# Attention steps two at a time beside an MLP: a changed instruction order on TensorE

## The chip, the cores and the metric

The kernel runs on one core of a Trainium2 chip. The metric is the time of one execution on the device in microseconds; the median of several runs counts. The core has five engines with an instruction queue each: TensorE (PE, matrix products into the eight banks of PSUM), VectorE (DVE), ScalarE (ACT), GpSimd (POOL) and SyncE (SP, which issues most DMAs). Each engine takes its instructions in their order; semaphores let it wait for the others.

## The reference

A linear attention with positive random features, and a gated MLP on what it gives. Cut to what matters (8 batches, 8 heads, 576 rows, head size 64, 128 features; 4608 rows of 512 into the MLP, which has 1536 inner columns):

```python
def phi(x):                       # x is q or k, scaled by 1/64**0.25
    proj = einsum('bhsd,md->bhsm', x, omega)
    h = proj - sum(x * x, -1, keepdims=True) / 2
    return exp(h - max(h, -1, keepdims=True)) / sqrt(m)
q_p, k_p = phi(q_s), phi(k_s)
kv = einsum('bhsm,bhsd->bhmd', k_p, v)
z = sum(k_p, axis=2)
x = einsum('bhsm,bhmd->bhsd', q_p, kv) / (einsum('bhsm,bhm->bhs', q_p, z)[..., None] + 1e-6)
x = x.transpose(0, 2, 1, 3).reshape(4608, 512)
g, val = x @ w_gate, x @ w_val
out = (g * sigmoid(g) * val) @ w_out
```

## The kernel before

**Attention.** q and k are cut into groups of 256 rows of a pair of heads (a batch has 8 such groups, and a ninth for the rows that are left over). A *step* takes two groups, mostly one of q and one of k; there are 72 steps. A step n goes through these functions, some of them one to three steps later:

- `st_transpose` turns the two groups on TensorE (tile `pt`, four transposes, in the bank of `ps_tr`); ACT copies the result to `x`, POOL squares the rows (`sq`).
- `st_project` multiplies by omega: eight matmuls into the two banks `pp0` and `pp1`, a bank for each head of the pair (L464). All float32 matmuls that are no transposes leave two records in the trace, so `pp` shows 16 records for a step.
- `st_max` takes sums and maxima on DVE (`st`), `st_exp` the exponentials on ACT (`ph`, eight instructions, which read `pp0` and `pp1`).
- `k_accumulate` adds the k group of two steps before to `kvacc` (one bank); when a half batch is complete, `kv_finalize` copies it to `kvr`. For batches from 4 on it also turns the sums z (`zp`, in the bank of `ps_att`), which go to DRAM and come back spread over the partitions (`load_z`).
- q of batches 0 to 3: `q_transpose` (`ptq`, copied to `qt`), `q_mult` (`po` = features times kv; DVE divides into `xn`), `q_out` (`xt`, two transposes of `xn`).
- q of batches 4 to 7: `q_den` (POOL and DVE: the denominators), `q_norm` (POOL: features divided), `q_transpose`, `q_out` (`xt`, matrix products of kv and `qt`, no transpose of `xn`).
- `q_out` ends with copies of `xt`: into the MLP's input tiles, or for later row tiles to DRAM (`xo`, then `xs`).

**MLP.** `stream` yields it in groups of matmuls on float32r numbers, each 128x512, split into high and low parts: 12 for a `g` or `v` bank, 9 for an `o` bank. They use three banks (`ps_moe`). Behind the attention a second stage follows (`pair_rounds`, seven products for eight) with other PSUM pools. All other time of the weights' conversion (`convert_all`, "ticks") lies on ACT, DVE, POOL and SP.

**PSUM.** Of eight banks the MLP has three, `ps_proj` two, `ps_att`, `ps_tr` and `kvacc` one each.

**Order.** The code is written as a loop over steps; a scheduler then puts the instructions of each engine in an order of its own by priority (the place in the program) and by when it takes operands and buffers to be ready, so the order on an engine isn't that of the code. For the first 25 steps (`EARLY`) the list `CLOSE` gives the order of the functions; there is no MLP work yet. From step 25 on it is the list `GROUPED`: attention functions, with `SHARE` at six places, where a share of the MLP groups that are due in this step is given out. `course` says how much MLP is due at which step.

Of the kernel before, what the change touches and what calls it, by code (L numbers as in the profile page):

```python
# [11 lines left out]
F32 = mybir.dt.float32  # L12
# [12 lines left out]
def kernel(  # L25
# [404 lines left out]
    def st_transpose(n):  # L430
# [12 lines left out]

        st = att.tile([P, 4, 2, CH, 2], F32, name=f"st_{n}", tag="st", bufs=6)
        sq = att.tile([P, 2, CH, 2, D], F32, name=f"sq_{n}", tag="sq")
# [12 lines left out]
    def st_project(n):  # L458
        if n >= NS:
            return  # L460
        x, st, sq = sts[n]

        new = ps_moe if n < EARLY and n % 2 else ps_proj
        pp = [new(f"pp{hh}_{n}", [P, 2, CH, M]) for hh in range(2)]  # L464
        for i in range(2):
            for c in range(CH):
                for hh in range(2):
                    r = slice(hh * D, (hh + 1) * D)
                    matmul(
                        pp[hh][:, i, c, :], x[r, i, c * P : (c + 1) * P], omT[r], start=True, stop=True  # L470
                    )
        sts[n] = st, sq, pp
        return True
# [44 lines left out]
    def kv_finalize(b, a2):  # L518
        acc = kvacc.pop((b, a2))
        raw = att.tile([P, 4, VW], F32, name=f"kvr{b}_{a2}", tag="kvr", bufs=4)  # L520
        nc.scalar.copy(raw, acc)  # L521
        for j in range(2):
            kvst[b, 2 * a2 + j] = raw[:, 2 * j : 2 * j + 2, :]
        if b >= BPOOL:

            zp = ps_att(f"zp{b}_{a2}", [4, P])
            transpose(zp, raw[:, :, D], ident)
            zs = att.tile([4, P], F32, name=f"zs{b}_{a2}", tag="zs")
# [5 lines left out]
    zds = {}  # L534
    zbc = {}
# [14 lines left out]
    def q_den(n):  # L550

        n -= JLAG
        for _, b, g, gr in slots(n, "q"):
# [10 lines left out]
            else:  # L564
# [4 lines left out]
                )  # L569
            dn = att.tile([P, 3, CH, 2], F32, name=f"dj{b}_{g}", tag="dj", bufs=6)  # L570
            nc.vector.tensor_reduce(dn[:, 0], jk, axis=AX.X, op=ALU.add)  # L571
# [63 lines left out]
    def q_mult(n):  # L635

        n -= MLAG
        for _, b, g, gr in slots(n, "q"):
# [17 lines left out]
            nc.vector.reciprocal(dn[:, 1], dn[:, 0])  # L656
            xn = att.tile([P, CH, 2, D], F32, name=f"xn{b}_{g}", tag="jx")
            nc.vector.tensor_tensor(
# [14 lines left out]
    def q_out(n):  # L673
        n -= OLAG
        for i, b, g, gr in slots(n, "q"):
            po = (ps_att if n + OLAG < EARLY or i else ps_tr)(f"xt{b}_{g}", [P, G])
            first = column(b, gr)
# [4 lines left out]
            else:  # L682
# [3 lines left out]
                for pr, o, w in segs:  # L686
                    for hh in range(2):
                        matmul(
                            po[hh * D : (hh + 1) * D, o : o + w], kvst[b, pr][:, hh, 0:D], qt[:, hh, o : o + w],
                            start=True, stop=True, skip_group_check=True,  # L690
                        )
            j, o = tile_of(first)
            if gr is None:
# [17 lines left out]
            if gr is None or gr[0] == NPAIR - 1:  # L711
                cols_done[0] = first + (RES if gr is None else G)
        return bool(slots(n, "q"))

# [405 lines left out]
    def turn_next(n):  # L1120
# [48 lines left out]
    ends = []  # L1169
    for n in range(NN):  # L1170
        if loaded <= n + LA:
# [6 lines left out]
        if n == FIRST_RAW:  # L1178
            load_raw(0)
        want = OPS * np.interp(clock[n + 1], [clock[m] for m, _ in marks], [x for _, x in marks])  # L1180
        order = CLOSE if n < EARLY else GROUPED
        left = len(order) if n < EARLY else order.count(SHARE)
        for what in order:
            with ExitStack() as es:
                if n < EARLY:
                    for ins in ends if what is st_project else ends[:1]:
                        es.enter_context(tc.issue_after(ins.ins))
                if what is not SHARE:
                    what(n)
            if n < EARLY:  # L1190
                if what is st_project:
                    ends.clear()
                ends.append(newest_pe[0])
            if what is turn_next and n < 2:
                warm(2, turned_in[0])
            if n < EARLY or what is SHARE:
                due = course[n + 1] - given[0] - debt[0]
                if due > 0:
                    give(due / left)
                for _ in range(int(np.ceil((want - ticks[0]) / left))):  # L1200
                    tick()
                left -= 1
        load_z(n)
    late.close()
    for name, pool in (
# [39 lines left out]
```

## Time and profile before

| | |
|---|---|
| runs (3) | 1166.57 to 1167.58 us, median 1166.86 us |
| profiled execution | 1166.82 us, span from first to last instruction 1165.0 us |
| mean granted TensorE clock | 0.997 of full |
| instructions in the trace | 18915 |
| DMA | 114.30 MB, mean 98 GB/s |

The profile page gives the busy time of each engine, the groups of instructions and the chain of work that ended last. The timeline lists instructions in order of time: start in microseconds from the span's start, duration, engine, line, operation, output and inputs, count, and in brackets how long the engine was idle before it and what ended that. TensorE's durations overlap with the next instruction's, so a piece of work there is measured from its start to the start of the next.

### The profile page before, as it was taken

Reading aid. Unit: us, or ns where it says so; the run is one execution under the profiler, and the core shown is the slowest. Engines: PE = TensorE matmul, PEld = TensorE weight load, DVE = VectorE, ACT = ScalarE, POOL = GpSimd, SP = SyncE. Lnnn points to the kernel's source line nnn. Section 1 sums busy time; section 2 is a strip of 40 time slices with the busy share of each in tenths; the row PEclk is TensorE's granted clock in tenths of the full one; section 3 lists DMA queues with packets and bytes.
Section 4 is the critical chain, followed back from the end, with each engine's and each line's share of the span. In section 5 each row is a group of like instructions: output and inputs, shape, how many; then the busy total and the mean of one; then the engine's idle time right before and its main releaser. Section 6 shows DMA issues by size and latency. Waiting matters only on the chain.

```text
span 1165.0 us, 18915 instructions
## 1 busy us (share of the span) xinstructions
PE 1137.2 (98%) x6645; PEld 939.5 (81%) x6646; DVE 707.4 (61%) x1289; ACT 678.3 (58%) x1539; POOL 615.5 (53%) x559
## 2 busy tenths in 40 slices
PE   8999999999999999989999999999999999999998
PEld 6888888888878778867788778888878888888886
DVE  5787667455656656565474566665566666456654
ACT  5887886876776866757434544454544445444441
POOL 5664433344556675587245555544455543455551
PEclk9999999999999999999999999999999999999999
DMA  6764445655445642322544111124211111211103
GB/s 137 179 160 114 128 142 161 178 135 143 122 126 137 168 132 78 114 68 65 154 118 126 46 55 55 55 74 122 59 55 55 54 37 46 81 55 55 46 19 72
DMA packets 173966, 114.30 MB, mean 98 GB/s; under 512 B 125840, under 2 KB 144304, under 8 KB 173872
## 3 DMA queue, kind: packets, MB, share of 16 engines
q1 hardware_dynamic: 172528, 112.78, 35.5%
q8 instruction: 52, 0.85, 0.3%
q10 hardware_dynamic: 1344, 0.33, 0.1%
q14 instruction: 42, 0.34, 0.1%
HBM read 87.88 MB, written 25.18 MB: 97 GB/s over the span
## 4 chain that ended last, share of the span: by engine, by line
PE 74%; DVE 10%; ACT 6%; POOL 4%; DMA 3%; issue 2%; SPq 1%; ACTq 0%; POOLq 0%; DVEq 0%
PE o L103 22%; PE a L103 16%; PE c L103 8%; PE g L103 6%; PE pp L103 4%; PE v L103 4%; PE d L103 4%; PE kvacc L103 3%; ACT ph L505 3%; PE ptq L107 2%; PE po L103 2%; PE pt L107 2%; PE xt L103 1%; DVE st L490 1%; POOL wlo L264 1%
## 5 line engine op out<-in xcount | busy, mean ns | idle before, releaser
L505 ACT ACTIVATE ph<-pp,st 128x128 f32<-128x128 f32 x576 | 157.8, 386 | 26.5 <-DVE st L493 26.0
L763 DVE TENSOR_TENSOR acc<-o,acc 128x512 f32<-128x512 f32 x156 | 105.8, 684 | 94.6 <-PE o L103 94.3
L446 POOL TENSOR_TENSOR sq<-nat 128x512 f32<-128x512 f32 x72 | 78.2, 1086 | 130.5 <-DVE st L483 89.1
L950 POOL TENSOR_TENSOR wlo<-wspare,whi 128x512 fp32r<-128x512 f32 (+1 forms) x60 | 61.0, 1037 | 117.4 <-ACT whi L949 111.0
L490 DVE TENSOR_REDUCE st<-pp 128x4 f32<-128x512 f32 x144 | 92.5, 683 | 39.0 <-PE pp L103 38.7
L264 POOL TENSOR_TENSOR wlo<-wraw,whi 128x512 fp32r<-128x512 f32 x59 | 82.7, 1406 | 26.7 <-ACT whi L263 22.8
L103 PE MATMUL pp<-omT,x 64*128 64x128 f32 x1152 | 87.3, 285 | 3.2 <-ACT x L454 2.2
L103 PEld LDWEIGHTS pp<-omT,x 64*128 64x128 f32 x1152 | 72.6, 187 | 20.2 <-issue 11.2
L950 POOL TENSOR_TENSOR wlo<-s,whi 128x512 fp32r<-128x512 f32 x64 | 82.6, 1311 | 3.8 <-ACT whi L949 3.8
L1059 ACT COPY late<-a 128x512 f32<-128x512 f32 x72 | 42.2, 586 | 59.7 <-PE a L103 58.5
L103 PE MATMUL o<-whi,late 128*128 128x512 f32 x192 | 74.5, 389 | 0.0
L571 DVE TENSOR_REDUCE dj<-jk 128x4 f32<-128x512 f32 x36 | 24.6, 684 | 73.5 <-POOL jk L567 60.6
L103 PE MATMUL kvacc<-v,ph 128*128 128x65 f32 x512 | 65.9, 268 | 0.5 <-ACT kvr L521 0.5
L824 POOL TENSOR_TENSOR hl<-sl,hh 128x512 fp32r<-128x512 f32 x36 | 47.0, 1308 | 34.8 <-ACT hh L823 34.7
L103 PEld LDWEIGHTS kvacc<-v,ph 128*128 128x128 f32 x512 | 63.1, 192 | 0.8 <-ACT kvr L521 0.6
L1063 DVE TENSOR_TENSOR late<-c,late 128x512 f32<-128x512 f32 x25 | 17.3, 692 | 69.7 <-PE c L103 60.6
L103 PE MATMUL g<-xh,whi 128*128 128x512 f32 x144 | 59.4, 412 | 0.0
L103 PE MATMUL o<-whi,hh 128*128 128x512 f32 x144 | 58.5, 406 | 0.1
L303 POOL TENSOR_TENSOR wc<-st 128x512 int32<-128x512 int32 x36 | 37.5, 1042 | 39.6 <-DVE st L298 17.2
L103 PE MATMUL v<-xh,whi 128*128 128x512 f32 x144 | 57.9, 402 | 0.0
L103 PE MATMUL g<-xh,wlo 128*128 128x512 f32 x144 | 57.7, 401 | 0.0
L103 PE MATMUL g<-xl,whi 128*128 128x512 f32 x144 | 57.2, 397 | 0.0
(261 smaller groups left out, 3369.4 us busy)
## 6 DMA issues: line engine op xcount, KB each, us to landing
wraw<-wscr SPq DMA_DIRECT2D x63, 256.0 KB, 2.7
wspare<-wscr SPq DMA_DIRECT2D x60, 256.0 KB, 2.8
wscr<-wc SPq DMA_DIRECT2D x36, 256.0 KB, 2.2
out_dram<-acc SPq DMA_DIRECT2D x72, 128.0 KB, 2.4
nat<-in_k_dram SPq DMA_DIRECT2D x64, 128.0 KB, 3.0
nat<-in_q_dram SPq DMA_DIRECT2D x64, 128.0 KB, 3.1
v<-in_v_dram SPq DMA_DIRECT2D x62, 128.0 KB, 3.5
st<-in_moe_w_gate_dram SPq DMA_DIRECT2D x12, 512.0 KB, 4.1
```

Source lines behind the costliest of these rows:

```text
L103: newest_pe[:] = [nc.tensor.matmul(*args, **kw)]
L107: newest_pe[:] = [nc.tensor.transpose(*args, **kw)]
L264: nc.gpsimd.tensor_tensor(lo, raw, hi.bitcast(F32), op=ALU.subtract)
L303: nc.gpsimd.tensor_tensor(ui, ri, low, op=ALU.add)
L446: nc.gpsimd.tensor_tensor(sq, nat, nat, op=ALU.mult)
L490: nc.vector.tensor_reduce(st[:, 1, :, :, hh], pp[hh], axis=AX.X, op=ALU.max, negate=True)
L505: step_end["s"] = nc.scalar.activation(ph[:, c, hh * M : (hh + 1) * M], pp[hh][:, i, c, :], AF.Exp, bias=st[:, 3, i, c, hh : hh + 1], scal ...
L571: nc.vector.tensor_reduce(dn[:, 0], jk, axis=AX.X, op=ALU.add)
L763: nc.vector.tensor_tensor(a_, po, a_, op=ALU.add)
L824: nc.gpsimd.tensor_tensor(hl, h, hh.bitcast(F32), op=ALU.subtract)
L950: nc.gpsimd.tensor_tensor(lo, src_, hi.bitcast(F32), op=ALU.subtract)
L1059: newest["s"] = nc.scalar.copy(keep[name], ps)
```

## The change

From step 25 on the loop goes over two steps at a time with one list, `DOUBLE`, whose entries are a function and which of the two steps it is called for. Its head puts together: `q_out` of both steps (`q_out_both`, two groups in one bank of `ps_moe`), `st_project` of both steps, `k_accumulate` of both. Behind it come the other functions, with `SHARE` at ten places: the transposes (`q_transpose`, `st_transpose`) now stand between MLP groups. The projections of the first step go to the banks of `ps_att` and `ps_tr`, those of the second to `ps_proj`, so that four banks hold them. `zp` gets a function of its own (`z_rows`), called behind two shares. Buffers: `st` and `dj` 4 for 6, `zs` 1 for 2, `xn` gets a tag of its own. In `CLOSE` the extra `q_out` of step 24 goes, and the transposes of step 26 are called there.

```diff
-        new = ps_moe if n < EARLY and n % 2 else ps_proj
-        pp = [new(f"pp{hh}_{n}", [P, 2, CH, M]) for hh in range(2)]
+        if n < EARLY:
+            new = (ps_moe, ps_moe) if n % 2 else (ps_proj, ps_proj)
+        else:
+            new = (ps_proj, ps_proj) if (n - EARLY) % 2 else (ps_att, ps_tr)
+        pp = [new[hh](f"pp{hh}_{n}", [P, 2, CH, M]) for hh in range(2)]
...
         if b >= BPOOL:
-
+            zraw[b, a2] = raw
+    def z_rows():
+        for (b, a2), raw in zraw.items():
             zp = ps_att(f"zp{b}_{a2}", [4, P])
             transpose(zp, raw[:, :, D], ident)
...
     def q_out(n):
-        n -= OLAG
-        for i, b, g, gr in slots(n, "q"):
-            po = (ps_att if n + OLAG < EARLY or i else ps_tr)(f"xt{b}_{g}", [P, G])
+        place_out([(g_, (ps_att if n < EARLY else ps_tr)(f"xt{g_[1]}_{g_[2]}", [P, G])) for g_ in slots(n - OLAG, "q")])
+    def q_out_both(n):
+        groups = slots(n - 1 - OLAG, "q") + slots(n - OLAG, "q")
+        at = []
+        for k_, g_ in enumerate(groups):
+            if k_ % 2 == 0:
+                two = ps_moe(f"xt{g_[1]}_{g_[2]}", [P, 2, G])
+            at.append((g_, two[:, k_ % 2]))
+        place_out(at)
...
-        lambda n: n == EARLY - 1 and q_out(n),
         lambda n: n == EARLY - 1 and q_mult(n),
+        lambda n: n == EARLY - 1 and st_transpose(n + 2),
...
-    GROUPED = (
-        q_out,
-        st_project,
-        q_transpose,
-        lambda n: k_accumulate(n, 0),
-        lambda n: k_accumulate(n, 1),
-        st_max,
-        st_exp,
-        q_den,
-        lambda n: st_transpose(n + 1),
-        SHARE, SHARE, SHARE,
-        lambda n: q_norm(n + 1),
-        q_mult,
-        SHARE, SHARE, SHARE,
-    )
+    DOUBLE = (
+        (q_out_both, 0),
+        (st_project, 0),
+        (st_project, 1),
+        (lambda n: k_accumulate(n, 0), 0),
+        (lambda n: k_accumulate(n, 1), 0),
+        (lambda n: k_accumulate(n, 0), 1),
+        (lambda n: k_accumulate(n, 1), 1),
+        (st_max, 0), (st_exp, 0), (q_norm, 0),
+        SHARE, SHARE,
+        (lambda n: z_rows(), 0), (load_z, 0), (load_z, 1),
+        (q_transpose, 0),
+        (st_max, 1), (st_exp, 1), (q_den, 0),
+        SHARE, SHARE,
+        (st_transpose, 2), (q_norm, 1), (q_mult, 0),
+        SHARE, SHARE, SHARE,
+        (q_transpose, 1), (st_transpose, 3), (q_den, 1),
+        SHARE, SHARE,
+        (q_mult, 1),
+        SHARE, SHARE, SHARE,
+    )
...
+    for n in range(EARLY, NN, 2):
+        loads(n)
+        loads(n + 1)
+        left = DOUBLE.count(SHARE)
+        last = min(n + 2, NN)
+        for what in DOUBLE:
+            if what is not SHARE:
+                what[0](n + what[1])
+                continue
+            share(course[last] - given[0] - debt[0], wanted(last), left)
+            left -= 1
```

What this makes of the order on TensorE, at three places. First the end of the projections of step 47. In the kernel before (`pp` the projection, `ptq` and `pt` the transposes, `v_4` an MLP group):

```order
L103 MATMUL pp_47_4314<-omT,x_4268 128x128
L103 MATMUL pp_47_4315<-omT,x_4268 128x128
L107 MATMUL ptq_3_4324<-ident,ph_45_4137 128x128 x4
L103 MATMUL kvacc_1_4127<-v_102,ph_45_4142 128x65 x4
L107 MATMUL pt_4356<-ident,nat_4088 128x128 x4
L103 MATMUL v_4_4372<-xh_1327,whi_1_3437 128x512
```

In the changed kernel eight rows of `pp_47` are followed by eight of `pp_48`; the last two of these and what follows:

```order
L103 MATMUL pp_48_4325<-omT,x_4258 128x128
L103 MATMUL pp_48_4326<-omT,x_4258 128x128
L103 MATMUL kvacc_1_4126<-v_102,ph_45_4145 128x65 x4
L103 MATMUL kvacc_1_4126<-v_103,ph_46_4193 128x65 x4
L103 MATMUL v_4_4365<-xh_1327,whi_1_3434 128x512
L103 MATMUL v_4_4365<-xl_1328,whi_1_3434 128x512
```

The transposes have left the stretch, and the accumulation of two steps stands in it. Second, where the transposes of the pair of steps 59 and 60 went, inside the MLP groups `o_2_0` and `o_2_1` (TensorE, changed kernel):

```order
L103 MATMUL o_2_0_5728<-wlo_2_5496,hh_8_5560 128x512
L103 MATMUL o_2_0_5728<-whi_2_5495,hl_8_5561 128x512
L107 MATMUL ptq_7_5741<-ident,ph_58_5453 128x128 x4
L103 MATMUL o_2_1_5771<-whi_2_5487,hh_6_5470 128x512
L103 MATMUL o_2_1_5771<-wlo_2_5488,hh_6_5470 128x512
L107 MATMUL pt_5748<-ident,nat_5577 128x128 x4
L103 MATMUL o_2_1_5771<-whi_2_5487,hl_6_5471 128x512
L103 MATMUL o_2_1_5771<-whi_2_5491,hh_7_5517 128x512
```

The same `ptq_7` and its neighbours before the change, at the end of the stretch of step 60:

```order
L107 MATMUL ptq_7_5712<-ident,ph_58_5543 128x128 x4
L103 MATMUL kvacc_0_5618<-v_98,ph_58_5548 128x65 x4
L107 MATMUL pt_5747<-ident,nat_5496 128x128 x4
L103 MATMUL o_2_0_5763<-whi_2_5460,hh_6_5443 128x512
L103 MATMUL o_2_0_5763<-wlo_2_5461,hh_6_5443 128x512
L103 MATMUL o_2_0_5763<-whi_2_5460,hl_6_5444 128x512
```

`ptq_7` now stands between two MLP groups, and `pt` inside one. Third, the first use of a bank of the first projection behind the stretch of steps 33 and 34 (TensorE, changed kernel; `ptq_8` goes to the bank of `ps_att`, which `pp_33` held):

```order
L103 MATMUL kvacc_0_2584<-v_98,ph_31_2599 128x65 x4
L103 MATMUL kvacc_0_2584<-v_99,ph_32_2637 128x65 x4
L103 MATMUL o_0_0_2859<-whi_2_2010,hh_0_2701 128x512
L103 MATMUL o_0_0_2859<-wlo_2_2011,hh_0_2701 128x512
L103 MATMUL o_0_0_2859<-whi_2_2010,hl_0_2702 128x512
L107 MATMUL ptq_8_2832<-ident,ph_32_2632 128x128 x4
L103 MATMUL o_0_0_2859<-whi_2_2064,hh_1_2736 128x512
```

Before, the same transposes followed the projection of step 33 at once, into a bank that no projection uses:

```order
L103 MATMUL pp_33_2773<-omT,x_2696 128x128
L107 MATMUL ptq_8_2782<-ident,ph_32_2681 128x128 x4
L103 MATMUL kvacc_0_2671<-v_98,ph_31_2581 128x65 x4
L107 MATMUL pt_2808<-ident,nat_2533 128x128 x4
L103 MATMUL o_0_0_2830<-whi_2_2036,hh_0_2703 128x512
```

Three MLP matmuls and the accumulation of two steps are now what stands between the projections and the next user of the bank.

More of the change, by code (lines that the diff above doesn't have):

```diff
@@ L524, in kv_finalize @@
         if b >= BPOOL:
+            zraw[b, a2] = raw
+    zraw = {}
+    zds = {}
+    def z_rows():
+        for (b, a2), raw in zraw.items():
             zp = ps_att(f"zp{b}_{a2}", [4, P])
             transpose(zp, raw[:, :, D], ident)
-            zs = att.tile([4, P], F32, name=f"zs{b}_{a2}", tag="zs")
+            zs = att.tile([4, P], F32, name=f"zs{b}_{a2}", tag="zs", bufs=1)
             nc.scalar.copy(zs, zp)
@@ L532, in kv_finalize @@
             zds[b, a2] = zd
-    zds = {}
+        zraw.clear()
     zbc = {}
@@ L569, in q_den @@
                 )
-            dn = att.tile([P, 3, CH, 2], F32, name=f"dj{b}_{g}", tag="dj", bufs=6)
+            dn = att.tile([P, 3, CH, 2], F32, name=f"dj{b}_{g}", tag="dj", bufs=4)
             nc.vector.tensor_reduce(dn[:, 0], jk, axis=AX.X, op=ALU.add)
@@ L656, in q_mult @@
             nc.vector.reciprocal(dn[:, 1], dn[:, 0])
-            xn = att.tile([P, CH, 2, D], F32, name=f"xn{b}_{g}", tag="jx")
+            xn = att.tile([P, CH, 2, D], F32, name=f"xn{b}_{g}", tag="xn")
             nc.vector.tensor_tensor(
@@ L673, in q_out, with place_out @@
     def q_out(n):
-        n -= OLAG
-        for i, b, g, gr in slots(n, "q"):
-            po = (ps_att if n + OLAG < EARLY or i else ps_tr)(f"xt{b}_{g}", [P, G])
+        place_out([(g_, (ps_att if n < EARLY else ps_tr)(f"xt{g_[1]}_{g_[2]}", [P, G])) for g_ in slots(n - OLAG, "q")])
[7 more added lines that the diff above has]
+        place_out(at)
+    def place_out(at):
+        for (i, b, g, gr), po in at:
             first = column(b, gr)
@@ L691, in q_out @@
                         )
+        for (i, b, g, gr), po in at:
+            first = column(b, gr)
             j, o = tile_of(first)
@@ L1134 @@
         q_den,
-        lambda n: n == EARLY - 1 and q_out(n),
         lambda n: n == EARLY - 1 and q_mult(n),
+        lambda n: n == EARLY - 1 and st_transpose(n + 2),
     )
-    GROUPED = (
-        q_out,
-        st_project,
-        q_transpose,
-        lambda n: k_accumulate(n, 0),
-        lambda n: k_accumulate(n, 1),
-        st_max,
-        st_exp,
-        q_den,
-        lambda n: st_transpose(n + 1),
+    DOUBLE = (
[6 more added lines that the diff above has]
+        (lambda n: k_accumulate(n, 1), 1),
+        (st_max, 0),
+        (st_exp, 0),
+        (q_norm, 0),
+        SHARE,
+        SHARE,
+        (lambda n: z_rows(), 0),
+        (load_z, 0),
+        (load_z, 1),
+        (q_transpose, 0),
+        (st_max, 1),
+        (st_exp, 1),
+        (q_den, 0),
+        SHARE,
+        SHARE,
+        (st_transpose, 2),
+        (q_norm, 1),
+        (q_mult, 0),
         SHARE,
@@ L1150 @@
         SHARE,
-        lambda n: q_norm(n + 1),
-        q_mult,
+        (q_transpose, 1),
+        (st_transpose, 3),
+        (q_den, 1),
+        SHARE,
+        SHARE,
+        (q_mult, 1),
         SHARE,
@@ L1169, with loads @@
     ends = []
-    for n in range(NN):
+    def loads(n):
+        nonlocal loaded
         if loaded <= n + LA:
@@ L1179, with share, wanted @@
             load_raw(0)
[L1180 to L1183, printed above, removed]
-            with ExitStack() as es:
[L1185 to L1193, printed above, removed]
+    def share(due, want, left):
+        if due > 0:
+            give(due / left)
+        for _ in range(int(np.ceil((want - ticks[0]) / left))):
+            tick()
+    def wanted(n):
+        return OPS * np.interp(clock[n], [clock[m] for m, _ in marks], [x for _, x in marks])
+    for n in range(EARLY):
+        loads(n)
+        for at, what in enumerate(CLOSE):
+            with ExitStack() as es:
+                for ins in ends if what is st_project else ends[:1]:
+                    es.enter_context(tc.issue_after(ins.ins))
+                what(n)
+            if what is st_project:
+                ends.clear()
+            ends.append(newest_pe[0])
             if what is turn_next and n < 2:
                 warm(2, turned_in[0])
[L1196 to L1202, printed above, removed]
-        load_z(n)
+            share(course[n + 1] - given[0] - debt[0], wanted(n + 1), len(CLOSE) - at)
+        load_z(n)
+    for n in range(EARLY, NN, 2):
+        loads(n)
+        loads(n + 1)
[7 more added lines that the diff above has]
+            left -= 1
     late.close()
```

3 lines of the change are left out of this document (1 added, 2 removed).

## The prediction

> **What bounds the kernel now.** I read the page first, then the stretches of time, then TensorE's waits, then its timeline.
>
> ```profile
> PE 1137.2 (98%) x6645; PEld 939.5 (81%) x6646; DVE 707.4 (61%) x1289; ACT 678.3 (58%) x1539; POOL 615.5 (53%) x559
> PE 74%; DVE 10%; ACT 6%; POOL 4%; DMA 3%; issue 2%; SPq 1%; ACTq 0%; POOLq 0%; DVEq 0%
> ```
>
> TensorE is busy for 98% of the span, and 74% of the chain that ended last lies on it. No other engine is over 61%. So what counts is how many microseconds TensorE's own row of instructions takes, and how long it waits.
>
> ```profile
> 110.00:564.00 454.00, 441.71 (x3030) 359.11 (x3030) 267.69 (x569) 326.00 (x789) 253.43 (x223) 1.00 0.45 125
> ```
>
> This is the stretch from 110 to 564 us (busy time of PE, PEld, DVE, ACT, POOL). By the order of the instructions, TensorE's rows are the same before and after the change up to a place at 110 us and again from 24 MLP matmuls behind 564 us on. So the change is worth what happens in the 454 us between. ACT, the next engine there, is busy for 326 of them (72%): it has room on the mean, not at each moment.
>
> ```profile
> PE ptq L107 <- ACT xo L703: 2.9, 4, 2.1
> PE xt L107 <- DVE xn L658: 2.3, 2, 1.2
> PE zp L107 <- ACT kvr L521: 2.0, 3, 1.1
> PE pt L107 <- ACT qt L633: 1.9, 1, 1.9
> ...
> PE pt L107 <- DVE xl L710: 0.2, 1, 0.2
> ```
>
> TensorE's waits in that stretch are nine groups; these are the four largest (9.1 us) and the last, and all nine come to **12.1 us**. The largest belong to attention steps that wait for a copy out of a PSUM bank.
>
> **What a step costs now.** This is TensorE's timeline around one step whose output is a matrix product (start, duration):
>
> ```profile
> 401.82 0.39 PE L103 MATMUL o<-whi,hl 128*128 128x512 f32 x1
> 402.14 0.65 PE L103 MATMUL xt<-qt,kvr 128*64 128x256 f32 x4
> 402.72 1.16 PE L103 MATMUL pp<-omT,x 64*128 64x128 f32 x16
> 403.82 0.66 PE L107 MATMUL ptq<-ident,ph 128*128 128x128 f32 x4
> 404.31 1.00 PE L103 MATMUL kvacc<-v,ph 128*128 128x65 f32 x8
> 405.15 0.61 PE L107 MATMUL pt<-ident,nat 128*128 128x128 f32 x4
> 405.51 0.47 PE L103 MATMUL o<-whi,hh 128*128 128x512 f32 x1
> 405.83 0.39 PE L103 MATMUL o<-wlo,hh 128*128 128x512 f32 x1
> 406.05 0.39 PE L103 MATMUL o<-whi,hl 128*128 128x512 f32 x1
> ```
>
> Durations overlap, so I count from start to start. MLP matmuls follow each other at 0.22 to 0.23 us (405.83 to 406.05); I take 0.227. From 401.82 to 405.83 are 4.01 us with two MLP matmuls in them, so the step costs 4.01 - 0.45 = 3.56, two steps 7.12. Of one step, 0.09 goes to the entry (0.32 instead of 0.23 from the last MLP matmul to xt) and 0.09 to the exit (0.32 for the first one behind pt).
>
> **The change part by part.** Merged pieces have neighbours in this trace:
>
> ```profile
> 557.38 1.08 PE L103 MATMUL xt<-qt,kvr 128*64 128x256 f32 x8
> 558.39 0.50 PE L103 MATMUL g<-xh,whi 128*128 128x512 f32 x1
> ...
> 163.74 0.71 PE L103 MATMUL pp<-omT,x 64*128 64x128 f32 x6
> 164.37 0.44 PE L107 MATMUL xt<-ident,xn 128*128 128x128 f32 x2
> 164.74 0.93 PE L103 MATMUL pp<-omT,x 64*128 64x128 f32 x10
> 165.60 0.66 PE L107 MATMUL ptq<-ident,ph 128*128 128x128 f32 x4
> ...
> 166.45 0.48 PE L103 MATMUL o<-whi,hh 128*128 128x512 f32 x1
> ...
> 306.63 1.00 PE L103 MATMUL kvacc<-vrest,ph 128*128 128x65 f32 x8
> 307.44 0.48 PE L103 MATMUL o<-whi,hl 128*128 128x512 f32 x1
> 307.75 0.39 PE L103 MATMUL o<-whi,hh 128*128 128x512 f32 x1
> ...
> 540.60 0.40 PE L103 MATMUL o<-whi,hl 128*128 128x512 f32 x1
> 540.84 0.60 PE L107 MATMUL ptq<-ident,ph 128*128 128x128 f32 x4
> 541.19 0.48 PE L103 MATMUL o<-whi,hh 128*128 128x512 f32 x1
> 541.51 0.39 PE L103 MATMUL o<-wlo,hh 128*128 128x512 f32 x1
> ```
>
> - *Two outputs in one stretch.* Eight xt records take 1.01 us (557.38 to 558.39); two times four took 1.16.
> - *Two projections in one stretch.* No 32 pp records stand together now. The first 16 cost 1.10 (402.72 to 403.82). Six cost 0.63 and ten 0.86, so a further record costs 0.23 / 4 = 0.058 and 16 more 0.92. Bounds are 0.92 and 1.10; I take 0.92, the nearer row, since the pieces differ in count alone.
> - *kvacc.* 0.84 in front of a transpose and 0.81 in front of an MLP matmul (306.63 to 307.44), so 1.65 for two: nothing gained. Its exit costs 0.31 - 0.23 = 0.08.
> - *The transposes go out of the stretch.* ptq and pt of a step cost 0.49 + 0.36 now. Alone between MLP matmuls four of them cost 0.35 (540.84 to 541.19) plus 0.01 at the entry and 0.09 at the exit: 0.45. The joined ptq and pt at 165.60 take 0.85 plus 0.10. So 0.45 for each four, apart or joined, and 1.80 for two steps.
>
> Two steps after: 0.09 + 1.01 + 1.10 + 0.92 + 0.84 + 0.81 + 0.08 + 1.80 = 6.65, against 7.12: **0.47 less**. With the upper bound on pp it is 0.29. There are 12 such pairs (steps 45 to 68): 5.6 us, at least 3.5.
>
> Steps 25 to 44 (10 pairs) have outputs that are transposes of xn, and their po products stay as they are. One of these steps:
>
> ```profile
> 228.74 0.39 PE L103 MATMUL v<-xh,wlo 128*128 128x512 f32 x1
> 228.97 0.38 PE L107 MATMUL xt<-ident,xn 128*128 128x128 f32 x2
> ...
> 232.39 0.39 PE L103 MATMUL v<-xl,whi 128*128 128x512 f32 x1
> ```
>
> 3.65 - 0.45 = 3.20, twice 6.40. After: the four xt transposes 0.31 as today (228.97 to the pp at 229.28) and half of 0.45 for two more, 0.53; then pp 2.02, kvacc 1.65, exit 0.08, transposes 1.80: 6.08. **0.32 less**, ten times: 3.2 us, at least 1.4. The last four pairs have hardly any projection left; I count 0.5 for them, between 0 and 1.
>
> TensorE's own work falls by 5.6 + 3.2 + 0.5 = **9.3 us** (5 to 10).
>
> *What the waits become.* The first projection's two banks are those that zp, ptq and pt of the same pair write next (ps_att and ps_tr have one buffer each). How long are they held?
>
> ```profile
> 403.92 1.29 DVE L490 TENSOR_REDUCE st<-pp 128x4 f32<-128x512 f32 x2 [0.98 <-PE pp L103]
> 405.44 0.17 DVE L493 SCALAR_TENSOR_TENSOR st<-st 128x8 f32<-128x8 f32 x1
> ...
> 406.28 2.18 ACT L505 ACTIVATE ph<-pp,st 128x128 f32<-128x128 f32 x8
> ```
>
> From the end of pp: two maxima and the bias until 405.61 (1.7 us), then eight exponentials in 2.18: 3.9 us, or about 3.4 for the first bank, whose last reader is the sixth. TensorE fills this with the second projection (0.92) and kvacc (1.65), which leaves 0.8 to 1.3 us, four to six MLP matmuls. In the changed order most pairs have nine or more there. Those of steps 33 (three), 51 (five), 57 (four) and 67 (six, with half the kvacc) have fewer, and wait by up to 0.5 each: 1 to 2 us. Behind a waiting zp or ptq stands all of TensorE's row. Where ACT is late with a copy of qt or x behind the second step's exponentials, the next transpose waits as the nine groups above show; with fewer places in the tail I expect fewer of those, and at step 25, where two pairs of po and xt now follow each other without MLP matmuls in between, one more. I take 11 us for 12.1, **1 us less**; bounds are 5 and 25.
>
> What is at nothing:
>
> ```profile
> nat<-in_k_dram SPq DMA_DIRECT2D x64, 128.0 KB, 3.0
> ```
>
> On SP two steps' q, k and v loads are now issued together, in front of the writes of xo. A load lands 3.0 us after its issue and its pt stands half a pair of steps later (a pair is two steps of 3.56 and the MLP matmuls between), so it is hidden; without that cover it would be 3 us for a pair. The xt pair now takes one of the MLP's three banks; its copies end while pp and kvacc (3.7 us) run, and no MLP matmul asks for a bank there. The silu/exp table loads fall from 42 to 34 rows on ACT, off TensorE's row.
>
> The profiled execution took 1166.82 us (span 1165.0), the median of the runs is 1166.86, so its sum holds for both: 1166.8 - 9.3 - 1 = 1156.5, say **1157 us**.
>
> **The rivals.**
>
> *The waits shrink too.* The two rows on steps behind ACT's xo and qt copies (4.8 us) and the xn row (2.3) come from tight places; pairs could have room at all of them. Then 12.1 falls to about 6: 1166.8 - 9.3 - 6 = 1151.5. For it: two steps' transposes are apart now. Against: what the next case says of the order.
>
> *The waits eat the gain.* By the order 23 blocks of transposes and 4 zp now interrupt an MLP group, which means that they stand just behind their operands. The rows of ptq on xo, zp on kvr and pt on qt are 8 waits with 6.8 us, 0.85 each. If a third of the 27 places waits so, that is 9 x 0.85 = 7.7 more: 1166.8 - 9.3 + 7.7 = 1165.2.
>
> *Slower: single banks.* If the hold of 3.9 us is not covered, because the MLP matmuls meant for it themselves wait or ACT is 1 us late, a pair waits by about 1.3 us in front of its first ptq or zp. Over the 22 pairs this is 29 us; if half of them do it, 14.5: 1166.8 - 9.3 + 14.5 = 1172. It decides from the point where the added waits exceed 9.3 us, so at seven or eight pairs. Against it stands the order, with nine or more MLP matmuls at most pairs. [...] With no overlap at all the sum would be 1166.8 - 9.3 + 29 = 1186; no run here shows that yet.
>
> A wait can also cost twice:
>
> ```profile
> 424.75 0.27 PE L107 MATMUL zp<-ident,kvr 128*4 128x128 f32 x1 [1.14 <-ACT kvr L521]
> ...
> 426.00:428.00 2.00, 2.00 (x7) 0.50 0.48 108
> ```
>
> Behind this wait the granted clock was 0.50, and seven matmuls took 2 us in place of 1.6 in this slice; each such event costs so much on top of the wait. [...]
>
> That the change does not do what it says is not open: the order shows the joined rows.
>
> **How the numbers follow.** The forecast has 0.50, the shrunken waits 0.22, waits that eat the gain 0.15, single banks 0.13. The best of both bounds at once is 1166.8 - 10 - 7 = 1150, the worst 1166.8 - 5 + 13 = 1175; the range is 1149 to 1171, which takes in the first three cases and leaves out the fourth and the worst of the bounds. A difference of 0.2% (2.3 us) is about what can be told from no change. Faster takes the first two and 0.02 of the third: 0.74; the same 0.13; slower 0.13.
>
> **What would show it.** Right: xt x8 at 1.0, pp x32 near 2.0, transposes between MLP matmuls, waits near 11 us between 110 us and the last xt, and that last xt some 10 us earlier. Wrong: pp x32 at 2.2, or wait rows of zp, ptq or pt on "ph" (exponentials) at most pairs, or clock rows of 0.50 at several places.

## The result, and the profile after

The changed kernel takes **1173.7 us** (median of 6 runs, 1171.34 to 1179.6) against 1166.71 for the kernel before, measured beside it: ratio 1.0069, 95% interval 1.0046 to 1.0092. It is slower by 7 us, and the forecast of 1157 with its range of 1149 to 1171 missed it. The profiled execution took 1175.89 us (span 1174.1), 9.1 us more than the profiled one of before.

The page of the changed kernel, first the engines' busy time, then the chain that ended last:

```profile
PE 1136.5 (97%) x6646; PEld 941.1 (80%) x6646; DVE 711.4 (61%) x1289; ACT 664.5 (57%) x1531; POOL 613.4 (52%) x559
PE 73%; DVE 10%; ACT 7%; POOL 3%; issue 3%; DMA 2%; SPq 1%; POOLq 0%; ACTq 0%; DVEq 0%
```

TensorE's busy time fell by 0.7 us while the span grew by 9.1. So TensorE stands still longer, and a part of its busy time must be slow.

To see how much of each, I take the same work out of both traces: from the first projection of step 24 to the start of the MLP matmul that has 1110 MLP matmuls ahead of it. In it are all attention products from step 24 on, and the change moves nothing over its ends. The stretch of before, then of after (columns as in the rows of stretches in the prediction: length, then busy time and records of PE, PEld, DVE, ACT, POOL, then the granted clock):

```profile
107.13:576.10 468.97, 456.68 (x3116) 371.82 (x3116) 274.55 (x584) 333.61 (x807) 254.92 (x225) 1.00 0.46 126
```

```profile
107.92:582.59 474.67, 454.61 (x3115) 373.08 (x3115) 274.55 (x579) 317.39 (x795) 251.72 (x225) 0.99 0.44 122
```

Length minus PE busy is TensorE's *idle* time: 12.3 before, 20.1 after. From the busy time I take off half of what was busy in slices with a granted clock of 0.50 (*clock loss*: one slice of 3.41 us before, four after; in the one before, MLP matmuls start 0.43 us apart, at 425.85 and 426.28, instead of 0.23); what remains is the *work* at full clock. With the time ahead of the stretch and behind it:

| profiled execution, us | ahead | idle | clock loss | work | behind | span |
|---|---|---|---|---|---|---|
| before | 107.1 | 12.3 | 1.7 | 455.0 | 588.9 | 1165.0 |
| after | 107.9 | 20.1 | 6.4 | 448.2 | 591.5 | 1174.1 |
| difference | +0.8 | **+7.8** | **+4.7** | **-6.8** | **+2.6** | +9.1 |

The joined rows did save work. What was lost is idle time, clock (the half-clock slices from 365.5, 406.4 and 532.7 us, in or behind waits of 2.7, 1.9 and 3.1 us), and 2.6 us in a place where I had looked for nothing.

TensorE's waits up to the last xt, by what ended them (total, times, longest); in all 19.7 us in 21 waits, against 12.1 in 17; the five largest groups:

```profile
PE ptq L107 <- issue: 6.4, 3, 3.1
PE ptq L107 <- POOL wlo L264: 2.7, 1, 2.7
PE ptq L107 <- ACT ph L508: 1.9, 3, 1.1
PE kvacc L103 <- ACT kvr L524: 1.9, 5, 0.7
PE xt L103 <- ACT qt L643: 1.9, 2, 1.6
```

The largest are waits of ptq. "issue" and "POOL wlo" aren't causes: these ptq stand ready with their operands and wait for the bank that the first projection holds until its exponentials are done. Each of the four starts 0.10 us behind the end of the sixth exponential, the last one that reads this bank. In all, nine waits of ptq and zp end 0.05 to 0.10 us behind a sixth exponential; together they are **12.5 us**, where the kernel before has none. All other waits come to 7.2, against 12.1 before. One such place on TensorE:

```profile
268.67 2.06 PE L103 MATMUL pp<-omT,x 64*128 64x128 f32 x32
270.65 2.00 PE L103 MATMUL kvacc<-v,ph 128*128 128x65 f32 x16
272.46 0.48 PE L103 MATMUL o<-whi,hh 128*128 128x512 f32 x1
...
274.39 0.39 PE L103 MATMUL o<-whi,hl 128*128 128x512 f32 x1
275.91 0.66 PE L107 MATMUL ptq<-ident,ph 128*128 128x128 f32 x4 [1.13 <-ACT ph L508]
```

The same time on DVE and on ACT:

```profile
269.86 1.29 DVE L493 TENSOR_REDUCE st<-pp 128x4 f32<-128x512 f32 x2 [1.90 <-PE pp L103]
...
271.39 0.17 DVE L496 SCALAR_TENSOR_TENSOR st<-st 128x8 f32<-128x8 f32 x1
```

```profile
272.56 0.32 ACT L725 COPY xo<-xt 128x192 f32<-128x192 f32 x1 [3.19 <-DMA xs<-xo]
272.90 1.28 ACT L508 ACT_TABLE_LOAD   x1
274.20 2.17 ACT L508 ACTIVATE ph<-pp,st 128x128 f32<-128x128 f32 x8
```

The bias is ready at 271.56, 1.8 us behind the first 16 projection records, as I had worked out. But the exponentials start at 274.20: ACT stands at the fourth xo copy of the pair, since the buffer that it takes, one of three, is still being written to DRAM, and then loads a table. Nine MLP matmuls aren't enough then, and TensorE waits although the pair is one of those that I had called covered.

The wait at 405.0 us (1.9) has an xo copy ahead of it in the same way. At the three other long waits, which end at 365.1, 442.6 and 533.5 us (2.7, 1.5 and 3.1), something else is late. ACT's rows ahead of their exponentials:

```profile
362.82 0.62 ACT L263 CAST whi<-wraw 128x512 fp32r<-128x512 f32 x1 [4.88 <-DMA wraw<-wscr]
363.35 2.17 ACT L508 ACTIVATE ph<-pp,st 128x128 f32<-128x128 f32 x8
...
439.54 1.28 ACT L508 ACT_TABLE_LOAD   x1 [2.38 <-DVE st L496]
...
530.49 1.28 ACT L508 ACT_TABLE_LOAD   x1 [3.87 <-DVE st L496]
```

At the first, a cast of the MLP's weights stands ahead and waits 4.9 us for their DMA; the bias had been ready at 361.09. At the other two DVE has the bias ready only 4.1 and 4.2 us behind the first projection, and then a table is loaded. So of these five waits with 10.3 us, two with 3.0 go back to xo.

### The profile page after: what moved, and what is told of

The parts are those of the page before. It is cut to its first block, busy times and chain, and to the rows that moved or that the text cites. A ratio compares the mean times of both kernels' runs of the same rounds, so it can differ in the third digit from the quotient of the medians.

```text
span 1174.1 us, 18910 instructions
## 1 busy us (share of the span) xinstructions
PE 1136.5 (97%) x6646; PEld 941.1 (80%) x6646; DVE 711.4 (61%) x1289; ACT 664.5 (57%) x1531; POOL 613.4 (52%) x559
## 4 chain that ended last, share of the span: by engine, by line
PE 73%; DVE 10%; ACT 7%; POOL 3%; issue 3%; DMA 2%; SPq 1%; POOLq 0%; ACTq 0%; DVEq 0%
PE o L103 22%; PE a L103 16%; PE c L103 8%; PE v L103 5%; PE g L103 5%; PE d L103 4%; PE pp L103 3%; ACT ph L508 3%; PE kvacc L103 3%; PE po L103 2%; PE ptq L107 2%; PE pt L107 2%; DVE st L493 2%; PE xt L103 1%; ACT L508 1%
## 5 line engine op out<-in xcount | busy, mean ns | idle before, releaser
L103 PE MATMUL pp<-omT,x 64*128 64x128 f32 x1152 | 79.3, 281 | 1.7 <-ACT x L454 1.7
L103 PEld LDWEIGHTS pp<-omT,x 64*128 64x128 f32 x1152 | 69.6, 187 | 12.2 <-issue 7.2
L1080 ACT COPY late<-a 128x512 f32<-128x512 f32 x72 | 42.2, 586 | 60.1 <-PE a L103 58.8
L103 PE MATMUL o<-whi,hl 128*128 128x512 f32 x144 | 57.8, 401 | 0.0
L103 PE MATMUL o<-wlo,hh 128*128 128x512 f32 x144 | 57.7, 401 | 0.0
```

The costliest lines, as they stand in the source:

```text
L103: newest_pe[:] = [nc.tensor.matmul(*args, **kw)]
L1080: newest["s"] = nc.scalar.copy(keep[name], ps)
```

## The experiments

Each run's ratio is to the kernel before on the same chip, with its 95% interval.

**1. One share later** (`e1_later`).

```diff
         (q_norm, 0),
-        SHARE, SHARE,
+        SHARE, SHARE, SHARE,
         (lambda n: z_rows(), 0),
...
         (q_den, 0),
-        SHARE, SHARE,
+        SHARE,
```

> The changed kernel with one of its ten shares of MLP work moved: three instead of two stand ahead of zp and the first ptq, one instead of two behind q_den of the first step. Theory A (single banks: what the change loses are waits of zp, ptq and pt for the first projection's banks, held 4.8 to 5.3 us by the exponentials instead of the 3.9 I took): one share is some 1.4 us of MLP matmuls, so TensorE's waits from 110 to 575 us fall from 19.7 to about 12, some half-clock slices go with them, and the time falls by 6 to 10 us, to 1164 to 1168. Theory B (the joined rows themselves are dear, or the attention's late end): waits fall by less than 3 us and the time stays within 1171 to 1175.

(A pair has twelve shares, as the list shows; "ten" there and in the part on the change is a slip.) Measured: 1169.18, ratio 1.0019 (1.0008 to 1.003): 4.5 us below the changed kernel (medians measured apart). Idle 18.3, clock loss 1.6. The direction is A's: the waits for the first projection's banks fall from 12.5 to 10.3 us. But the idle time fell by 1.8 us, not by 7 or 8, and most of the gain of the profiled execution is that three of four slices at half clock are gone.

**2. One copy to xo** (`e2_xo_once`).

```diff
-            for src, pr, j, o, w in parts_:
-                if j in x_dram:
-                    xo = att.tile(list(src.shape), F32, name=f"xo{b}_{g}_{j}", tag="xo", bufs=3)
-                    nc.scalar.copy(xo, src)
-                    nc.sync.dma_start(x_dram[j][:, pr, o : o + w], xo)
+            if all(p_[2] in x_dram for p_ in parts_):
+                xo = att.tile([P, G], F32, name=f"xo{b}_{g}", tag="xo", bufs=3)
+                nc.scalar.copy(xo, po)
+                for src, pr, j, o, w in parts_:
...
+                    nc.sync.dma_start(x_dram[j][:, pr, o : o + w], from_)
```

> The changed kernel, but each output group is copied to xo by one ACT copy, also where it is cut between two tiles; only the DMA is cut. A pair then needs two xo buffers instead of up to four of three. Theory A1 (ACT stands in front of the exponentials because the fourth xo copy waits for a write to DRAM): ACT's wait xo <- DMA falls from 11.8 us to under 4, the TensorE waits at 274 and 402 us (1.3 and 2.0) go, one half-clock slice with them, and the time falls by 3 to 6 us. Rival (xo's wait is hidden behind the other causes of late exponentials): ACT's wait falls all the same and the time moves by less than 1.5 us.

Measured: 1168.05, ratio 1.0015 (1.0004 to 1.0026), 5.7 us less. ACT's wait for xo's writes in the changed kernel, and then in this one:

```profile
ACT xo L725 <- DMA xs<-xo: 11.8, 6, 3.2
```

```profile
ACT xo L724 <- DMA xs<-xo: 2.0, 2, 1.6
```

Idle 17.4, clock loss 1.6. The waits of TensorE at 274 and 402 us are gone, and those for the first projection's banks come to 9.8. A1 holds for these two places.

**3 and 4. No table loads** (`e3_no_silu`, `e4_no_silu_before`): silu replaced by a copy in the changed kernel and in the one before.

```diff
-                nc.scalar.activation(sl, pg[f], AF.Silu)
+                nc.scalar.activation(sl, pg[f], AF.Copy)
```

> The changed kernel with a plain copy in place of silu in the MLP's gates (the output is then that of a gate without silu), so that ACT never has to load a table between silu and exp. Theory A2 (table loads of 1.28 us in front of the exponentials are a large part of the hold): the hold of the first projection's banks falls from 4.8 to about 4, TensorE's waits from 110 to 575 us from 19.7 to 10 to 13, and the time by 6 to 12 us. Rival (loads lie beside other waits): waits 16 to 20, time within 3 us.

> The kernel before with the same plain copy in place of silu: the control for the run above. Theory A2: it gains little, 0 to 3 us, since its steps wait for exponentials less; the difference between the two kernels without table loads is then 0 to -6 us (changed kernel faster) instead of +7. Rival: it gains as much as the changed kernel, and the difference stays near +7.

Measured: 1168.63 (5.1 us below the changed kernel) and 1159.27 (ratio 0.9932, 0.9914 to 0.9949: 7.0 us below the kernel before). The loads cost the kernel before as much: its idle time falls from 12.3 to 6.7. So A2 falls as a cause of the *difference*, and the control was needed: the first of the two alone would have read as its proof.

**5 and 6. Both edits, and an earlier end** (`e5_later_xo`, `e6_later_xo_margin`). e5 has the edits of e1 and e2; e6 has these and:

```diff
-    MARGIN = 45.0
+    MARGIN = 51.0
```

> Both edits of the first two runs (a share more ahead of the first ptq, xo copied once) in the changed kernel. Alone they took 4.5 and 5.7 us off it (1173.7 to 1169.2 and 1168.0). Theory A (waits for single banks, with ACT's row ahead of the exponentials as their cause): the causes differ in place, the waits at 274 and 402 us go in both and those at 362 and 437 us shrink further, so the sum is nearly kept: 1164 to 1167, TensorE's waits before the last xt at 14 to 17 us against 23.6, no or one half-clock event there. Rival (both remove the same waits): no better than the better one, 1167.5 to 1170.

> The same, and the planner's margin at the end of the attention raised from 45 to 51 us, so that the last xt stands behind 1056 MLP matmuls as in the kernel before, not behind 1080. Theory C (the late end of the attention, 24 MLP matmuls, costs 2.8 us behind the last xt, by new waits at 594 and 603 us): 2 to 3 us less than the run above, 1161.5 to 1165, faster than both kernels. Rival (the waits behind the last xt come from elsewhere, or the denser attention loses as much): within 1 us of the run above.

(The 23.6 there comes from another count, of distances between starts on TensorE. By the view of waits the changed kernel has 19.7, e5 14.3 and e13 18.2.) Measured: 1165.34, ratio 0.9985 (0.9977 to 0.9994), and 1186.54, ratio 1.0171 (1.0155 to 1.0187). With both edits idle is 14.8 and clock loss 1.7: A's causes add up, and of the 12.5 us that idle and clock had grown by, 10.0 are back. The waits for the first projection's banks fall to 6.9, the others stay at 7.4. The margin was a failure: against e5 idle +7.6, clock loss +6.8, work +6.9, and behind the stretch still 591.0. So C falls: the time behind the last xt doesn't come from the late end. Of the 6.9 more work, 5.5 are at the projections: in e6 six more pairs have their 32 pp records split into 8 or 10 and 22 or 24, with xt, kvacc or MLP between, and take about 2.9 us in place of 1.99. Why the scheduler splits them there stays open.

**7 and 8. A control, and outputs alone** (`e7_xo_once_before`, `e8_outputs_paired`). e7 is the second edit in the kernel before. e8 is the kernel before with this:

```diff
     GROUPED = (
-        q_out,
+        lambda n: (n - EARLY) % 2 == 0 and q_out_both(n),
         st_project,
```

> Control: the one copy to xo in the kernel before. Theory A1: there ACT waits for xo's writes 1.2 us in one place only, so the time stays within 1.5 us of 1166.5, and what the copy gives the changed kernel is a cost of the change. Rival (the copies are dear in any order, as the table loads proved to be): 3 to 6 us faster.

> A part of the change alone: the kernel before with the outputs of two q groups in one stretch and one MLP bank (every second step), projections and transposes as before. By the rows: 12 pairs save 0.15 (eight xt in 1.01 for 1.16) and one entry of 0.09, 10 pairs of xn transposes about one entry, together some 4 us; the attention ends 24 MLP matmuls later as in the whole change. Theory A with C: -4 + 2.8 = 1164 to 1167, and no waits for exponentials. Rival (a pair's xo copies, four behind each other, hold ACT as in the change): 1168 to 1171, waits behind ACT's xo.

Measured: 1166.34, ratio 0.9992 (0.9983 to 1.0002), and 1166.91, ratio 0.9998 (0.9989 to 1.0007). e7: what the one copy gives is a cost of the change; A1 stands. e8 has A's time, but not for A's reasons: its work falls by 6.8 us and not by some 4, and waits for exponentials are there (two of pp with 4.5 us, against 1.0 in the kernel before). Its account stands in the table below.

**9 to 12** (`e9_two_later`, `e10_fill_one_wait`, `e11_margin_before`, `e12_outputs_xo`). e9 is e5 with a fourth share ahead of zp and ptq, taken from the three at the end. e11 is the kernel before with the margin at 51. e12 is e8 with the one copy to xo. e10 is e5 with this ahead of the ptq of step 69:

```diff
+        if m == 69:
+            idb = ident.bitcast(BF16)
+            for _ in range(20):
+                nc.tensor.matmul(fill, idb[:, 0:P], idb[:, 0:248], start=False, stop=False, skip_group_check=True)
```

> The run with both edits (1165.3) and one more of a pair's twelve shares (some 1.2 us of MLP matmuls) moved from behind the last q_mult to the place ahead of zp and the first ptq: four shares there, two at the end. Theory A (single banks): the waits of zp and of the first ptq that are left (256, 361, 398, 433 us and the first part of 521: 7.7 us together) shrink by up to 1.2 each, so 3 to 5 us less: 1160.5 to 1162.5. Rival (what is left there is ACT and DVE being late as a whole, and the transposes behind now wait instead): 1164.5 to 1168, with new waits of po, pt or xt on qt.

> The run with both edits, and 20 small matmuls of the identity (bf16, 128x248; they write a corner of the kvacc bank that nothing reads) directly ahead of one block of transposes, the one that TensorE waits 2.4 us for at 521.6 us and behind which a slice at half clock follows in the changed kernel and in all three runs with its order kept. Theory D (a stretch of 3.41 us in which TensorE idles for about 2 us or more is followed by one at half clock, which costs up to 1.7 us on top of the wait): some 2.1 us of the wait are filled, the wait itself ends at the same time, no half-clock slice stands behind it, and the time is 1.0 to 1.7 us less, 1163.6 to 1164.4. Rival (the slice does not come from the wait): half clock at 525 us all the same, time 1165 to 1166.

> The kernel before with the planner's margin at 51 instead of 45 us, the edit that cost the changed kernel 21 us. Theory E (any new deal of the MLP work over the steps costs waits and half-clock slices, whatever the edit is for): 1172 to 1185, with three or more half-clock slices. Rival (the margin is harmless where steps stand singly; the changed kernel's order alone is sensitive): 1164 to 1169.

> The part alone that kept the time (the kernel before with outputs of two groups in one stretch, 1166.9), and with it the one copy to xo. Theory A1: the pp waits at 363 and 381 us (2.7 and 1.8, ended by exponentials that stand behind the pair's xo copies and wc) shrink: 1161 to 1165. Rival (the xo copies are not what ACT is late with there): 1166 to 1168.

*e9:* 1170.68, ratio 1.0036 (1.0023 to 1.0049), 5 us *worse* than e5. Its waits:

```profile
PE pt L107 <- ACT qt L643: 3.8, 2, 2.3
PE po L103 <- ACT qt L643: 3.5, 2, 3.1
PE pt L107 <- ACT x L454: 2.4, 3, 1.2
```

The rival's mechanism holds, at a time worse than it named. The waits for the first projection's banks fall from e5's 6.9 us to 2.1, as A says, but all others rise from 7.4 to 15.4: po and pt, which come behind, now wait for copies of qt and x (the three groups shown are 9.7 us, in e5 4.1). So A in its plain form (a share more, a wait less) is too simple: what is put ahead of one transpose is missing ahead of the next.

*e10:* 1167.47, ratio 1.0006 (0.9997 to 1.0015); e5 had 0.9985. The slices around the place, and the instructions that stood there:

```profile
521.00:524.40 3.40, 2.96 (x24) 2.25 (x22) 3.02 (x8) 2.98 (x8) 0.58 (x2) 1.00 0.01 2
524.40:527.80 3.40, 3.33 (x19) 2.85 (x20) 2.43 (x6) 3.37 (x7) 3.40 (x4) 1.00 0.00 0
```

```profile
521.67 2.29 PE L643 MATMUL kvacc<-ident 128*128 128x248 bf16 x20
524.47 1.14 PE L107 MATMUL ptq<-ident,ph 128*128 128x128 f32 x8 [0.50 <-issue]
...
532.90 0.63 PE L107 MATMUL ptq<-ident,ph 128*128 128x128 f32 x4 [1.86 <-ACT x L454]
```

The clock stays at 1.00 behind the filled wait, as D says. One execution doesn't prove it: e15, which is e5 again, has no slice at half clock there either (see the last section, where the counts speak for D). The time doesn't fall: the new rows shifted the scheduler's order, ACT runs a silu with two table loads ahead of the copy of x, and a later ptq waits 1.86 us, which it didn't in e5.

*e11:* 1165.98, ratio 0.9999 (0.999 to 1.0008). The rival holds: the margin is harmless to single steps. *e12:* 1167.79, ratio 1.0015 (1.0006 to 1.0024), the rival's time; idle fell to 12.1 from e8's 14.4, without a gain on the clock.

**13 to 15** (`e13_projections_paired`, `e14_projections_later_xo`, `e15_later_xo_again`). e13 is the changed kernel with single outputs, e14 the same with both edits, e15 is e5 again.

```diff
     DOUBLE = (
-        (q_out_both, 0),
+        (q_out, 0),
...
+        (q_out, 1),
         (q_transpose, 1),
```

> The other part of the change alone: projections, kvacc and transposes of two steps as in the changed kernel, but the outputs singly, each step's own, in one bank of the MLP's: the first at the head of the pair, the second ahead of the second ptq. The last xt then stands behind 1068 MLP matmuls, 12 later than in the kernel before. Theory A (the waits belong to the joined projections, whose banks the transposes need; outputs in pairs are what was worth having): 1172 to 1178, TensorE's waits before the last xt at 22 us or more, two or three half-clock slices, and 599.5 to 601 us behind the last xt plus 2.7 for 12 matmuls. Rival (the waits come from four output copies in a row on ACT): 1164 to 1168.

> The same with the two edits that helped the whole change (a share more ahead of the first ptq, xo copied once). Theory A: the later ptq helps here as there, some 4 us, the one copy less than there, since outputs stand singly: 1167 to 1172. Rival: 1162 to 1166, the best of all, because no output is late.

> The changed kernel with both edits once more, beside these two on one chip, since its gain of 0.15% is small and the run that filled a wait in it was measured on another chip. If the gain is real: 1163.5 to 1166.5 and a ratio whose interval lies below 1. If not: 1166 to 1168.

Measured: 1177.54 (1.0099, 1.0083 to 1.0114), 1174.48 (1.0077, 1.0063 to 1.009) and 1165.83 (0.9999, 0.999 to 1.0008). e13's time fits A, its waits don't: 18.2 us are below the 22, and 6.6 of them are for the first projection's banks. Four slices ran at half clock, one more than named, and the 599.8 us behind the last xt fit only without the 2.7 that were to be added. e14 gains 3 us by the edits and ends above A's upper bound. By e15 the gain of e5 over the kernel before isn't real beyond doubt; no version here surely beats both.

The two parts alone, with the rows of the stretch of e8 and then of e13 from which their accounts start:

```profile
105.51:573.17 467.66, 453.28 (x3115) 374.57 (x3115) 274.94 (x579) 331.17 (x803) 254.05 (x225) 0.99 0.44 123
```

```profile
107.42:586.45 479.03, 460.72 (x3115) 371.55 (x3115) 273.81 (x582) 321.06 (x801) 251.64 (x225) 0.99 0.45 122
```

| profiled execution, us | ahead | idle | clock loss | work | behind | span |
|---|---|---|---|---|---|---|
| before | 107.1 | 12.3 | 1.7 | 455.0 | 588.9 | 1165.0 |
| outputs in pairs alone (e8) | 105.5 | 14.4 | 5.1 | 448.2 | 591.9 | 1165.1 |
| projections in pairs alone (e13) | 107.4 | 18.3 | 6.5 | 454.2 | 590.0 | 1176.5 |
| both, the change | 107.9 | 20.1 | 6.4 | 448.2 | 591.5 | 1174.1 |
| the change, later and one copy (e5) | 107.4 | 14.8 | 1.7 | 448.4 | 591.5 | 1163.7 |
| the same kernel again (e15) | 107.2 | 15.1 | 0.0 | 448.6 | 592.3 | 1163.3 |
| before, one copy (e7) | 106.9 | 11.9 | 0.0 | 455.1 | 592.2 | 1166.1 |

That is the answer to where the time went. The whole gain in work, 6.8 us, is that of the outputs. The joined projections (with the transposes moved behind them) save 0.8 and cost 6.0 of idle time and 4.8 of clock. e5 and e15, one kernel, tell the scatter of such an account: 0.3 in idle and work, 0.8 behind, a whole slice of 1.7 in the clock. So idle and work of the two parts nearly add up to the change, and the clock loss (3.4 and 4.8 more, 4.7 in both) doesn't. Behind the stretch e8 has 3.0 more and e13 1.1; but e7, the kernel before with one copy to xo, has 3.3 more too (1.7 of it a half-clock slice), so this isn't a price of either part.

## Why the prediction was wrong

*TensorE's own work, 9.3 less (5 to 10).* Measured 6.8: inside the bounds. The most mis-sized term is kvacc. I took 1.65 for two behind each other; in the rows above 16 records take 1.81 (270.65 to 272.46). Over the whole stretch, start to start without idle and clock loss, kvacc takes 44.5 us for 42.2 before, where I had 0.7 less: 3.0 off, more than what is missing. Other terms came out better than forecast (pp 6.3 less for 4.0, xt 3.4 less for 2.7), so that the sum is this near is luck in part. It also tells why projections in pairs save nothing: in e13 pp takes 5.6 us less, but kvacc 2.2 and the MLP's rows 6.1 more, for there are more changes between MLP and attention (84 before, 115 in e13, 124 after, 73 in e8).

*Waits, 12.1 to 11.* **This step failed**, at "the hold of 3.9 us" and "most pairs have nine or more there". For pairs that aren't covered I had 1 to 2 us; the waits for the first projection's banks are 12.5. Of the four pairs that I named, three wait, and so do five that I called covered (steps 29, 39, 41, 55 and 59: 5.6 us); the pair of steps 69 and 70, at 533.5 us, adds 3.1.

I built the hold out of durations, 1.7 for DVE and 2.18 for the exponentials, as if ACT were free when the bias is ready; my own rows had the bias at 405.61 and the exponentials only at 406.28. Over the 22 pairs the sixth exponential, after which the first bank is free, ends 4.8 us behind the projection on the mean, at five pairs about 6 to 7. What stands ahead on ACT is in part what I had put under "at nothing": the xo copies, of which I had that they "end while pp and kvacc (3.7 us) run" (above, 272.88 against 272.46) and whose writes I had not looked at as what gives ACT its buffer back, and the table load, "off TensorE's row". The rest is the weights' cast that waits for its DMA and the biases that are late. e2 and e7 show the xo copies to be a cost of the change; e3 with e4 shows that the table loads cost the kernel before as much; the cast and the late biases were not tested by a run. Both edits together (e5) give back 5.3 of the 7.8 us of idle time. That I expected "fewer of those" was right for the other waits: 7.2 us for 12.1.

*"A wait can also cost twice."* The mechanism stood there with its row and was in no sum, and the row was misread: seven is the number of matmuls that touch the 2 us, of which each takes 0.43 instead of 0.23. By an estimate from these starts a slice of 3.41 us costs about 1.6 us, not 0.4. Four slices in place of one cost 4.7 us, more than half of what the idle time cost itself. Without this term and the next the measured parts would have stayed in the range: 1166.8 - 6.8 + 7.8 = 1167.8.

*"So the change is worth what happens in the 454 us between."* Behind the stretch are 2.6 us more. The rows there are alike, but not the times at which their operands come:

```profile
PE o L103 <- ACT sl L821: 1.2, 1, 1.2
...
PE v L103 <- DVE acc L784: 0.6, 1, 0.6
PE o L103 <- DVE acc L784: 0.4, 1, 0.4
```

These waits between the last xt and 700 us aren't in the profiled execution of before. e8 has all three (2.4 us), but e13 has 1.0 of them, and e7, with single outputs, one of 2.0 for `sl` and a half-clock slice behind it. So neither the late end (e6) nor the outputs in pairs explain them; the cause stays open.

*The rivals.* "Slower: single banks" named the place and the mechanism, with 0.13 of the chance. Its own price was near, too: 14.5 us for half of the 22 pairs, measured 12.5 at nine places. That its 1172 lies within 2 us of the result is luck in the rest: the other waits fell by 4.9 us, the work by 6.8 instead of the 9.3 that its sum has, and 4.7 of clock and 2.6 behind came on top. In e8, where no transposes need a projection's bank, idle grows by 2.1, in e13 by 6.0. The upper figure beside it, 1186 for a wait at all 22 pairs, is far off. *Signs:* of those named for "wrong", several slices at 0.50 came, and waits of ptq and zp for exponentials, though at nine places and not at most pairs; of those for "right", xt x8 at 1.0 and pp x32 near 2.0 came too, while the last xt came 12 us later and not 10 earlier.

## What to carry to other kernels

How long a bank is held isn't the sum of its readers' durations: it runs until the in-order queue of the reading engine gets there; here the sixth exponential ended 4.8 us behind the projection on the mean, where durations alone had given 3.4. So read from the trace what stands ahead (a copy that waits for a DMA to free its buffer, a cast that waits for its input, a table load, a bias that is late) and how late the last reader ends. Joining work on the busiest engine gives the other engines their work in lumps (here four xo copies of a pair on ACT, which in all waited 11.8 us for their writes), and parts of one change can have opposite signs: time them alone, and give each experiment its control in the kernel before. Idle time on TensorE cost more by the clock (here 4.7 us on top of 7.8); count such a cost in the sum where waits grow.

## What the runs showed of the hardware

*Slices at half clock, and how the waits lie to them.* Within each trace of this case, all slices at half clock begin at multiples of 3.413 us from each other (in that of the changed kernel 12, 49 and 50 of them behind the first). I laid this grid over the whole of the 17 traces: from 60 us on, all 15 slices of it in which TensorE idled for more than 2.0 us are followed by one at 0.50; of about 60 with 1.16 to 2.0 us of idle time 13 are; with less, 6 of about 5400 are, five of which ran at half clock already. (The bounds are chosen from these counts.) In the trace of the changed kernel the slices from 362.05, 403.01 and 529.31 us, with 2.72, 1.88 and 2.29 us of idle time, are followed by one at 0.50; those from 392.77 and 440.56, with 1.41 and 1.46, aren't. The same kernel has such a slice in one execution and not in the next. e5, and then e15, at the same wait of 2.4 us:

```profile
521.78:525.19 3.41, 1.01 (x9) 0.70 (x8) 2.24 (x7) 3.40 (x10) 1.30 (x2) 1.00 0.00 0
525.19:528.60 3.41, 3.41 (x12) 2.74 (x11) 2.54 (x6) 3.35 (x12) 3.41 (x4) 0.50 0.01 1
```

```profile
520.68:524.09 3.41, 1.57 (x7) 0.95 (x6) 3.31 (x8) 2.46 (x6) 0.63 (x1) 1.00 0.14 45
524.09:527.51 3.42, 2.84 (x17) 2.43 (x18) 2.21 (x6) 3.42 (x12) 3.38 (x3) 1.00 0.00 0
```

In e5 all of the 2.40 us lie in one slice, and the next runs at half clock; in e15 the wait is split into 1.84 and 0.57, and the clock stays. The last xt comes 1.3 us earlier there (563.9 and 565.2 us). e2's wait of 3.1 us at the same block of transposes is split into 1.84 and 1.25, and there the clock stays as well. The runs of the changed kernel, which spread over 8.3 us, fit this: the fastest has a mean granted clock of 0.998, the slowest of 0.993, and by an estimate from these 0.005 of 1174 us, 5.9 us, is the clock's share.

*Small DVE operations that lasted as long as one of POOL.* The bias takes 0.17 us at 271.39. At another pair of the changed kernel its two operations take 1.23 and 1.21. DVE there, and POOL:

```profile
436.99 1.23 DVE L495 SCALAR_TENSOR_TENSOR st<-st 128x8 f32<-128x8 f32 x1
438.25 1.21 DVE L496 SCALAR_TENSOR_TENSOR st<-st 128x8 f32<-128x8 f32 x1
```

```profile
436.92 1.27 POOL L264 TENSOR_TENSOR wlo<-wraw,whi 128x512 fp32r<-128x512 f32 x1
438.14 1.29 POOL L845 TENSOR_TENSOR hl<-sl,hh 128x512 fp32r<-128x512 f32 x1
```

Each of the two ends within 0.05 us of the POOL operation beside it. By an estimate from these durations it made the exponentials of that pair 2.1 us later, and its ptq (at 442.6 us) waits 1.5. It is no single case: in the 17 traces 357 of these operations (2448 in all, most at 0.17 us) last longer than 0.4 us, and every one of them ends within 0.06 us of the end of a POOL operation; in the traces of before and after it is 43 of 288, within 0.04 us. That POOL is the cause was not tested by a run.
